# Attention and a gated MLP on one core: plain fp32 scores for the first three pairs, decode steps on GpSimd, and another written order

## The chip, the cores and the metric

The kernel runs on one core of a Trainium2 chip. The metric is the device time in microseconds of one execution; a profiled execution also gives its span, which begins and ends a little inside that time. On a core, TensorE (PE in the profile, PEld for its weight loads), VectorE (DVE), ScalarE (ACT) and GpSimd (POOL) each work through their own list of instructions in order and wait for one another by semaphores; SyncE (SP) issues nearly all transfers.

## The reference

For 8 batches and 8 heads, q, k and v have 576 positions of 64 numbers. q and k are rotated by position, scores are softmaxed, and the values are weighted; the heads of a batch then form the rows of a gated MLP with a product over positions.

```python
q_rot, k_rot = rotate(q), rotate(k)          # x1*cos - x2*sin, x1*sin + x2*cos
scores = q_rot @ k_rot.T / sqrt(64)
attn = exp(scores - max) / (sum + 1e-9)
x = (attn @ v)  -> [batch, 576, 512]
h = relu(x @ w_in); u, v = halves of h
v_n = (v - mean) / sqrt(var + 1e-6)
gated = u * (w_spatial @ v_n + b_spatial)
out = gated @ w_out
```

The arrays w_in and w_out arrive as 64-bit floats, read as two 32-bit words.

## The kernel before

Work goes by pairs of heads, 32 in all, four to a batch. Every product that needs full precision is made of fp32r products (one instruction each) of a high part, a rounded copy, and a low part, the rest. The only plain fp32 products are those of the values.

A pair is prepared (`prepare`, lines 442 to 531): q and k (two tiles `st`) and v (`vr`) are loaded; q and k are multiplied by a rotation table (`rope`, L487; q and k have tables of their own, `tabs`, in different row orders) and summed (`rope_sum`, L491); ScalarE makes high parts (L370, `hq`; L503), VectorE or GpSimd low parts (L373, `lq`; L471, `lk`). Then transfers from SBUF to SBUF build stacks (`ks`, `qs`, `qz`) in which the high and the low part stand in the two halves of the rows, so that one product takes both. Twelve such transfers, 1.56 MB, belong to a pair.

`attention` (L535) makes nine score tiles of 128 rows (`scores`, tile number 8 holds the rest of both heads): four products a tile (six for tile 8), the row maximum on VectorE (`nmx`, L583), the exponential on ScalarE (`e`, L584), a transpose in blocks on VectorE (`tu`, L594). When all nine are there, the values (`pv`, L553) follow in three chunks of 48 products; the three together are called a session here. `tu` has one buffer, so the next pair's transposes wait for the end of a session. `normalise` brings the sums across by a small transfer (`rt`, `rb`) and writes the MLP's input `x`.

`mlp` makes four groups of products per batch, named `pa`, `pb`, `pc` and `pd`, which run between the scores and values of the next batch's pairs. `decode` (L378) turns a 512 KB block of 64-bit weights into a high and a low part, with six steps on VectorE and two on ScalarE; twelve blocks are decoded, early in the program.

The order on each engine isn't the order of the code. `Program.run` (L140) plays all operations through a list of costs, keys and buffer counts when the program is written, and writes each engine's instructions in the order in which that play starts them. Keys (`PREP`, `STAGE`, `DEC_V` and the like) and buffer counts (`SLOTS`) are the numbers that set it. Where TensorE has nothing in that play, up to a set time, `warm` (L803) writes an idle product of zeros.

## Time and profile before

| | us |
|---|---|
| runs, lowest, median, highest | 935.18, 938.51, 942.9 |
| profiled execution | 940.61 |
| its span | 938.8 |
| TensorE busy | 864.5 |
| VectorE busy | 599.9 |
| ScalarE busy | 484.7 |
| GpSimd busy | 483.1 |

A busy TensorE is not TensorE at its peak: matmuls overlap, warm products count, and part of the time the granted clock is lower. Shares over the whole span hide that the program has stages; the rows below are by stage. Pairs and tiles are counted from 0. "Scores of pair 6" start at 194.72 us: they are the first split products after 194.32 in the timeline, and the place of each pair was read by laying the written order of TensorE beside the timeline.

### The profile page before, as it was taken

What the parts mean: (1) busy time and instruction counts of PE and PEld (TensorE: products, weight loads), DVE (VectorE), ACT (ScalarE), POOL (GpSimd) and SP (SyncE); (2) the same over time, 40 slices, a digit from 0 to 9 for tenths busy, and PEclk for the clock granted to TensorE, in tenths of its full rate; (3) what the DMA queues carried; (4) which work ended last, traced back from release to release, by engine and by line L of the source; (5) the groups of instructions that cost most, each with busy time, mean ns of one, the idle gap of its engine ahead of it and who ended that gap; (6) DMA issues with size and microseconds to landing.
All of it is one profiled execution on the core that took longest, in us unless ns stands there. A gap on an engine that the chain in (4) does not pass through costs nothing.

```text
span 938.8 us, 32216 instructions
## 1 busy us (share of the span) xinstructions
PE 864.5 (92%) x13594; PEld 762.6 (81%) x13594; DVE 599.9 (64%) x1203; ACT 484.7 (52%) x1207; POOL 483.1 (51%) x467
## 2 busy tenths in 40 slices
PE   7879867789889999999999999999999899999998
PEld 4656546689788988889988998799888899898998
DVE  3868778767658775675758665777557565965121
ACT  1434436554446644575457555674457445753352
POOL 1744235865545664675645574467466464423131
PEclk9879859999999999999999999999999999999999
DMA  9977978677888777877887789777877769663101
GB/s 228 246 170 197 212 180 201 149 176 173 187 210 208 165 171 200 194 175 164 189 213 178 176 189 233 157 182 177 205 184 168 164 151 238 139 139 72 52 1 51
DMA packets 101682, 161.13 MB, mean 172 GB/s; under 512 B 29153, under 2 KB 47969, under 8 KB 101538
## 3 DMA queue, kind: packets, MB, share of 16 engines
q1 hardware_dynamic: 100882, 157.82, 70.7%
q8 instruction: 107, 1.75, 0.8%
q10 hardware_dynamic: 656, 1.25, 0.5%
q14 instruction: 37, 0.30, 0.1%
HBM read 98.08 MB, written 9.96 MB: 115 GB/s over the span
## 4 chain that ended last, share of the span: by engine, by line
PE 68%; DMA 18%; DVE 5%; issue 4%; SPq 3%; ACT 1%; ACTq 0%; DVEq 0%
PE sc L579 15%; PE pv L553 14%; PE pc L712 10%; PE pb L694 9%; PE pd L732 9%; PE pa L671 8%; PE warm L806 3%; DMA qz<-hq 3%; DMA qs<-hq 3%; SPq L367 3%; DMA vr<-in_v_dram 1%; DVE tu L594 1%; DVE nmx L583 1%; DMA ks<-st 1%; DMA wi10raw<-in_w_in_dram 1%
## 5 line engine op out<-in xcount | busy, mean ns | idle before, releaser
L583 DVE TENSOR_REDUCE nmx<-sc 128x1 f32<-128x576 f32 x288 | 212.8, 744 | 153.6 <-PE sc L579 146.4
L584 ACT ACTIVATE e<-sc,nmx 128x576 f32<-128x576 f32 x288 | 212.7, 739 | 186.3 <-DVE nmx L583 149.9
L594 DVE STREAM_TRANSPOSE tu<-e 128x576 f32<-128x576 f32 x288 | 213.8, 759 | 35.0 <-PE pv L553 28.9
L487 POOL TENSOR_TENSOR st<-st,tabs 128x576 f32<-128x576 f32 x123 | 172.2, 1422 | 73.8 <-DMA st<-in_qk_dram 41.7
L553 PE MATMUL pv<-tu,vr 32*64 32x144 f32 x9216 | 182.9, 291 | 25.9 <-issue 25.0
L553 PEld LDWEIGHTS pv<-tu,vr 32*64 32x64 f32 x9216 | 150.5, 132 | 50.8 <-issue 46.1
L579 PE MATMUL sc<-ks,qs 128*128 128x288 f32 x640 | 145.1, 317 | 40.9 <-DVE x L630 15.8
L579 PEld LDWEIGHTS sc<-ks,qs 128*128 128x128 f32 x640 | 107.8, 197 | 63.2 <-issue 33.9
L579 PE MATMUL sc<-lk,qz 128*128 128x288 f32 x576 | 129.2, 307 | 1.5 <-DMA qz<-hq 1.3
L712 PE MATMUL pc<-wsp,vn 128*128 128x288 f32 x768 | 125.2, 298 | 0.2 <-ACT u L697 0.2
L671 PE MATMUL pa<-wi,x 128*128 128x512 f32 x448 | 121.2, 401 | 0.0
L694 PE MATMUL pb<-x,wi 128*128 128x288 f32 x768 | 119.8, 300 | 0.1
L373 POOL TENSOR_TENSOR lq<-st,hq 128x512 fp32r<-128x512 f32 (+1 forms) x62 | 51.0, 846 | 130.9 <-ACT hq L370 130.8
L373 POOL TENSOR_TENSOR x<-x,x 128x64 fp32r<-128x64 f32 (+1 forms) x96 | 59.4, 649 | 109.3 <-ACT x L370 109.3
L694 PEld LDWEIGHTS pb<-x,wi 128*128 128x128 f32 x768 | 108.5, 190 | 4.9 <-issue 3.4
L712 PEld LDWEIGHTS pc<-wsp,vn 128*128 128x128 f32 x768 | 109.8, 189 | 3.0 <-issue 2.6
L732 PE MATMUL pd<-g,wo 128*128 128x288 f32 x744 | 110.7, 298 | 0.0
L732 PEld LDWEIGHTS pd<-g,wo 128*128 128x128 f32 x744 | 103.0, 190 | 1.7 <-issue 1.6
L579 PEld LDWEIGHTS sc<-lk,qz 128*128 128x128 f32 x576 | 96.4, 197 | 3.5 <-DMA qz<-hq 3.3
L671 PEld LDWEIGHTS pa<-wi,x 128*128 128x128 f32 x448 | 79.5, 189 | 16.3 <-issue 4.0
L373 POOL TENSOR_TENSOR g<-u,g 128x288 fp32r<-128x288 f32 x64 | 52.7, 824 | 75.2 <-ACT g L370 75.1
L491 POOL TENSOR_TENSOR st<-st 128x576 f32<-128x576 f32 x62 | 87.9, 1420 | 4.0 <-DVE st L487 1.6
(104 smaller groups left out, 777.0 us busy)
## 6 DMA issues: line engine op xcount, KB each, us to landing
vr<-in_v_dram SPq DMA_DIRECT2D x128, 320.0 KB, 6.3
st<-in_qk_dram SPq DMA_DIRECT2D x32, 576.0 KB, 4.5
ks<-st SPq DMA_DIRECT2D x128, 144.0 KB, 5.6
qs<-hq SPq DMA_DIRECT2D x64, 164.0 KB, 5.1
qs<-lq SPq DMA_DIRECT2D x64, 164.0 KB, 6.2
st<-in_qk_dram SPq DMA_DIRECT2D x32, 288.0 KB, 4.0
out_dram<-ob SPq DMA_DIRECT2D x31, 288.0 KB, 3.7
st<-in_qk_dram SPq DMA_DIRECT2D x32, 256.0 KB, 4.4
```

The lines of the kernel that those rows point to most:

```text
L373: eng.tensor_tensor(out=lo, in0=src, in1=hi.bitcast(F32), op=ALU.subtract)
L487: f = lambda e: e.tensor_tensor(out=st[j][:, cols], in0=st[j][:, cols], in1=tabs[j][:, cols], op=ALU.mult)
L491: f = lambda e: e.tensor_tensor(out=st[j][:, :S], in0=st[j][:, :S], in1=st[j][:, S:2 * S], op=ALU.add)
L553: nc.tensor.matmul(outs[g][64 * a:64 * a + 64], lhsT=vr[rows, NQ * (kb % 4) + kb // 4, a, :], rhs=tu[rows, kb, Q4 * a:Q4 * a + Q4], start= ...
L579: nc.tensor.matmul(pt[:, n_c * 512:n_c * 512 + HALF], lhsT=lhsT, rhs=rhs[:, n_c * HALF:n_c * HALF + HALF], start=(n == 0), stop=(n == len( ...
L583: op(DVE, 749, key + k_max, lambda: nc.vector.tensor_reduce(out=nmx.tile, in_=tops(pt), op=ALU.max, axis=AX.XY, negate=True), r=[pt], w=[n ...
L584: op(ACT, 920, key + k_exp, lambda: nc.scalar.activation(e.tile.rearrange("p (c n) -> p c n", c=2), tops(pt), AF.Exp, bias=nmx.tile, scale ...
L594: nc.vector.transpose(out=dst, in_=src)
L671: nc.tensor.matmul(pm[:, :HF], lhsT=lhsT, rhs=win[1, d][:, j, :], start=(d == 0 and n == 0), stop=(d == 3 and n == len(todo) - 1))
L694: nc.tensor.matmul(pm[:, :HALF], lhsT=win[0, d][:, i, f * P:(f + 1) * P], rhs=x[d][:, at:at + HALF], start=(d == 0 and n == 0), stop=(d == ...
L712: nc.tensor.matmul(pm[:, :HALF], lhsT=lhsT, rhs=rhs, start=(t == 0 and n == 0), stop=(t == 4 and n == 1))
L732: nc.tensor.matmul(pm[:, :HALF], lhsT=wout[d,][:, i, m * P:(m + 1) * P], rhs=gs[d][:, at:at + HALF], start=(d == 0 and n == 0), stop=(d == ...
```

## The change

The first three pairs make no high and low parts and no stacks: the sum of the rotation writes q in fp32 straight into `hq` or `lq` in turn (and the columns of tile 8 into a new tile `jq`), ScalarE scales k in place, and a score tile is two plain fp32 products. `decode` has four steps on VectorE, three on ScalarE and two that GpSimd takes. q and k use one table. Between the chunks of a session of the first six pairs stand ten products of zeros. The planner knows sizes of transfers, `stage` and `e` have four buffers, `x32` goes into `rb`, and nearly all keys have other values.

```diff
-    "stage": 3, "lk": 2, "vraw": 1, "e": 3, "tu": 1, "rb": 1, "x32": 1, "xg": 7, "m": 4,
+    "stage": 4, "lk": 2, "vraw": 1, "e": 4, "tu": 1, "rb": 1, "xg": 7, "m": 4,
-DEC_V = [-26.92, 52.32, 24.86, 22.99]
+DEC_V = [650.29, 522.41, -36.97, 219.03]
+DEC_DVE = [0.0, 0.0]
+PLAIN = 3
+FILL_PAIRS, FILL = 6, 10
-WARM_FROM, WARM_FULL, WARM_TO, WARM_NS, WARM_AFTER, WARM_COLS = 2500, 44958.22, 100000, 170, -0.15, 384
+WARM_FROM, WARM_FULL, WARM_TO, WARM_NS, WARM_AFTER, WARM_COLS = 2500, 44958.22, 200000, 170, -0.15, 384
...
+                    if e == DMA and item[2].kb in (512, 576) and moved > now + FULL:
+                        passed.append(item)
+                        heapq.heappush(events, (moved - FULL, n, "wake", None))
...
-    tabs = [T([P, 2 * S], F32, f"tabs{j}") for j in range(2)]
+    tab2 = T([P, 2 * S], F32, "tab2")
+    jq = T([P, 2, P], F32, "jq")
...
-        op(DVE, 640, key - DEC_ON, bits(0xFFFFF, 0x100000, ALU.bitwise_and, ALU.bitwise_or), r=[t1], w=[pt])
-        op(DVE, 640, key - DEC_ON, lambda: stt(out=pt.tile, in0=word(0, U32), scalar=2.0**-32, in1=ints(), op0=ALU.mult, op1=ALU.add), r=[t0], w=[pt])
-        op(DVE, 640, key - DEC_ON, lambda: stt(out=pt.tile, in0=pt.tile, scalar=2.0**-20, in1=sg.tile.bitcast(F32), op0=ALU.mult, op1=ALU.mult), r=[sg], w=[pt])
-        op(ACT, 480, key - DEC_ON, high, r=[pt], w=[t0, t1, (n, "hi")])
-        op(DVE, 640, key - DEC_ON, lambda: rest_lo(nc.vector, where[at][:, 1, :], pt.tile, where[at][:, 0, :]), r=[pt, (n, "hi")], w=[n])
+        op(DVE, 640, key - DEC_ON, lambda: ts(out=ints(), in0=word(1), scalar1=0xFFFFF, scalar2=None, op0=ALU.bitwise_and), r=[t1], w=[pt])
+        op(ACT, 500, key - DEC_ON, lambda: nc.scalar.activation(pt.tile, ints(), AF.Copy, bias=1.0, scale=2.0**-20), w=[pt])
+        op(DVE, 640, key - DEC_ON, lambda: stt(out=val.tile, in0=word(0, U32), scalar=2.0**-52, in1=pt.tile, op0=ALU.mult, op1=ALU.add), r=[t0, pt], w=[val], new=[val])
+
+        def product(e):
+            e.tensor_tensor(out=val.tile, in0=val.tile, in1=sg.tile.bitcast(F32), op=ALU.mult)
+
+        prog.either({POOL: pool_ns(HF), **({DVE: 640} if DEC_DVE[0] > key else {})}, key - DEC_ON, lambda e: product(vec[e]), r=[sg], w=[val])
+        op(ACT, 480, key - DEC_ON, high, r=[val], w=[t0, t1, (n, "hi")])
+        prog.either({POOL: pool_ns(HF), **({DVE: 640} if DEC_DVE[1] > key else {})}, key - DEC_ON, lambda e: rest_lo(vec[e], where[at][:, 1, :], val.tile, where[at][:, 0, :]), r=[val, (n, "hi")], w=[n])
...
+        def plain_sum(e):
+            add = lambda **kw: e.tensor_tensor(op=ALU.add, **kw)
+            (dst, _), (x0, y0), (x1, y1) = spread((hq, lq)[i % 2].bitcast(F32)), turned(), turned(S)
+            add(out=dst, in0=x0, in1=x1)
+            for a in range(2):
+                rows = slice(64 * a, 64 * a + 64)
+                add(out=jq[rows, i % 2].rearrange("p (g n) -> p g n", n=32)[:, :, 16 * a:16 * a + 16], in0=y0[rows], in1=y1[rows])
...
+        if i < PLAIN:
+            scaled = lambda: nc.scalar.activation(st[1][:, :S], st[1][:, :S], AF.Copy, scale=0.125)
+            op(ACT, 573, key - K_HIQ, scaled, w=[(st[1], 0)])
+            prepped[i] = (lk, vr, st[1], i % 2)
+            return
...
+            if i < FILL_PAIRS and n < CHUNKS - 1:
+                for _ in range(FILL):
+                    nc.tensor.matmul(pv[1][:, Q4:Q4 + WARM_COLS - 16], lhsT=zero[:, :P], rhs=zero[:, 16:], start=False, stop=False)
...
+            if kt:
+                pq = (hq, lq)[n_q].bitcast(F32)
+                rows = slice(0, P) if c == 8 else slice(64 * heads[0], 64 * heads[0] + 64)
+                parts = [(jq[:, n_q] if c == 8 else pq[rows, P * (c % 4):P * (c % 4) + P], kt[rows, :S])]
```

Because the order is planned, the change moves instructions everywhere. Three places follow. In the names the number behind a letter group is the pair, the batch or the weight block (`st1_0` is q of pair 1, `wi02` block 2 of the first half of w_in); the last number counts buffers.

SyncE's queue at the start of the program, before, behind the load of pair 0's q:

```order
L367 DMA st0_1_98<-in_qk_dram 128x1152
L367 DMA vr0_120<-in_v_dram 32x4x640 x4
L367 DMA wi10raw_182<-in_w_in_dram 128x1024
L352 DMA st1_0_220<-in_qk_dram 64x1152
L353 DMA st1_0_220<-in_qk_dram 64x2x512
L354 DMA st1_0_220<-in_qk_dram 64x2x64
L367 DMA ks_76<-st0_1_98 64x576 x2
L367 DMA qs_75<-hq_78 64x656
L367 DMA qz_77<-hq_78 64x656
L367 DMA qs_75<-lq_79 64x656 x2
```

After, in the same place:

```order
L371 DMA st0_1_102<-in_qk_dram 64x1152
L372 DMA st0_1_102<-in_qk_dram 64x2x512
L373 DMA st0_1_102<-in_qk_dram 64x2x64
L386 DMA vr0_124<-in_v_dram 32x4x640 x4
L371 DMA st1_0_157<-in_qk_dram 64x1152
L372 DMA st1_0_157<-in_qk_dram 64x2x512
L373 DMA st1_0_157<-in_qk_dram 64x2x64
L371 DMA st1_1_183<-in_qk_dram 64x1152
L372 DMA st1_1_183<-in_qk_dram 64x2x512
L373 DMA st1_1_183<-in_qk_dram 64x2x64
```

The stacks of pair 0 and the first weight have gone from here, and the q and k of pair 1 and the q of pair 2 (the next rows) are loaded ahead of any weight.

VectorE while the first pair ends, before, with steps of the decode of `wi00` and `wi13`:

```order
L405 TENSOR_SCALAR dcwi13_599<-wi13raw_524 128x512
L413 SCALAR_TENSOR_TENSOR dcwi00_489<-wi00raw_427,dcwi00_489 128x512
L594 STREAM_TRANSPOSE tu0_376<-e0_7_601 128x18x32
L633 RECIPROCAL sums0_67<-sums0_67 128x9
L414 SCALAR_TENSOR_TENSOR dcwi00_489<-dcwi00_489,sgwi00_544 128x512
L634 STREAM_TRANSPOSE rt0_689<-sums0_67 128x32
L411 SCALAR_TENSOR_TENSOR sgwi13_693<-wi13raw_524,dcwi13_599 128x512
L373 TENSOR_TENSOR wi00_691<-dcwi00_489,wi00_691 128x512
```

After, GpSimd during the session of pair 0, with the last steps of the decode of `wi02`, `wi12` and `wi03`:

```order
L509 TENSOR_TENSOR st2_1_366<-st2_1_366,tab2_63 128x576 x2
L524 TENSOR_TENSOR st2_1_366<-st2_1_366 128x576
L437 TENSOR_TENSOR vlwi02_557<-vlwi02_557,sgwi02_477 128x512
L437 TENSOR_TENSOR vlwi12_566<-vlwi12_566,sgwi12_552 128x512
L392 TENSOR_TENSOR wi02_644<-vlwi02_557,wi02_644 128x512
L392 TENSOR_TENSOR wi12_647<-vlwi12_566,wi12_647 128x512
L509 TENSOR_TENSOR st3_0_432<-st3_0_432,tab2_63 128x576
L437 TENSOR_TENSOR vlwi03_713<-vlwi03_713,sgwi03_642 128x512
L524 TENSOR_TENSOR st3_0_432<-st3_0_432 128x576
L392 TENSOR_TENSOR x0_746<-rb0_635,x0_746 128x512
```

The product with the sign and power (L414 before, L437 after) and the low part (L373 before, L392 after) have moved from VectorE to GpSimd, where they stand between the rotations and sums (L509, L524) of pairs 2 and 3.

TensorE between the first and the second chunk of the session of pair 13, before, from the last products of one chunk to the first of the next:

```order
L553 MATMUL pv13_1_6016<-tu13_5844,vr13_5829 64x144
L553 MATMUL pv13_2_6017<-tu13_5844,vr13_5829 64x144 x2
L694 MATMUL pb2_00_6008<-x9_4562,wi01_2141 128x288 x3
L579 MATMUL sc14_2_6085<-ks_76,qs_75 128x288 x2
L579 MATMUL sc14_2_6085<-lk14_5543,qz_77 128x288 x2
L694 MATMUL pb2_00_6008<-x10_5003,wi02_2295 128x288 x3
L553 MATMUL pv13_0_6015<-tu13_5844,vr13_5829 64x144
```

After, between the second and the third chunk of the same session:

```order
L593 MATMUL pv13_1_5972<-tu13_5813,vr13_5795 64x144
L593 MATMUL pv13_2_5973<-tu13_5813,vr13_5795 64x144 x2
L747 MATMUL pb2_01_6070<-x9_4544,wi01_1369 128x288 x3
L628 MATMUL sc14_1_6143<-ks_75,qs_74 128x288 x2
L628 MATMUL sc14_1_6143<-lk14_5528,qz_76 128x288 x2
L747 MATMUL pb2_01_6070<-x10_4967,wi02_644 128x288 x3
L747 MATMUL pb2_10_6157<-x8_4098,wi00_1062 128x288 x3
L747 MATMUL pb2_01_6070<-x11_5554,wi03_754 128x288 x3
L747 MATMUL pb2_10_6157<-x9_4544,wi01_1369 128x288 x3
L593 MATMUL pv13_0_5971<-tu13_5813,vr13_5795 64x144
```

The first chunk's scores are now those of tile 0 of the next pair (tile 2 before), tile 1 stands in the second space, and more of the MLP's products stand between two chunks: 13 in the first space and 19 in this one, 10 in each before.

## Rows read from the trace of the kernel before

**Rows 1.** Stages: us; busy PE, PEld, DVE, ACT, POOL; clock; DMA share; GB/s.
```profile
0.00:26.39 26.39, 17.01 (x91) 9.56 (x92) 9.84 (x16) 3.89 (x6) 5.48 (x16) 0.92 0.96 227
26.39:194.72 168.33, 136.19 (x1963) 101.59 (x1964) 130.72 (x236) 82.02 (x192) 87.96 (x77) 0.85 0.80 193
194.72:275.00 80.28, 70.68 (x1234) 64.91 (x1233) 50.95 (x93) 38.88 (x101) 41.10 (x39) 0.98 0.79 187
275.00:870.00 595.00, 575.23 (x9862) 524.00 (x9861) 395.94 (x815) 334.55 (x848) 333.85 (x320) 0.99 0.75 177
```

**Rows 2.** TensorE's timeline: start, us, line, operation, tiles, count, idle before.
```profile
26.39 0.82 PE L579 MATMUL sc<-ks,qs 128*128 128x288 f32 x2 [8.25 <-DMA qs<-lq]
...
194.72 0.46 PE L579 MATMUL sc<-ks,qs 128*128 128x288 f32 x2
195.02 0.48 PE L579 MATMUL sc<-lk,qz 128*128 128x288 f32 x2
195.34 2.56 PE L694 MATMUL pb<-x,wi 128*128 128x288 f32 x18
```

**Rows 3.** Chain of work that ended last, before the first scores.
```profile
9.62 10.74 DMA wi10raw<-in_w_in_dram
...
22.57 3.69 DMA qs<-lq
```

**Rows 4.** VectorE's timeline, the first rotations.
```profile
9.70 1.43 DVE L487 TENSOR_TENSOR st<-st,tabs 128x576 f32<-128x576 f32 x2 [8.62 <-DMA tabs<-in_tab_dram]
12.99 1.43 DVE L487 TENSOR_TENSOR st<-st,tabs 128x576 f32<-128x576 f32 x2 [1.87 <-DMA tabs<-in_tab_dram]
```

**Rows 5.** Groups of instructions over the span, shapes kept apart.
```profile
L594 DVE STREAM_TRANSPOSE tu<-e 128x576 f32<-128x576 f32 x288 | 213.8, 759 | 35.0 <-PE pv L553 28.9 <-ACT e L584 5.8
...
L583 DVE TENSOR_REDUCE nmx<-sc 128x1 f32<-128x576 f32 x288 | 212.8, 744 | 153.6 <-PE sc L579 146.4 <-ACT g L370 5.9
...
L373 POOL TENSOR_TENSOR vn<-vv,vn 128x512 fp32r<-128x512 f32 x32 | 41.4, 1306 | 38.1 <-ACT vn L370 38.1
...
L373 DVE TENSOR_TENSOR wi<-dcwi,wi 128x512 fp32r<-128x512 f32 x8 | 5.4, 677 | 0.0
...
L410 ACT ACTIVATE dcwi<-dcwi,bias 128x512 int32<-128x512 int32 x8 | 5.3, 661 | 9.0 <-DVE dcwi L405 8.9
```

**Rows 6.** The table by stretch, four stretches of the second stage.
```profile
26.39:51.93 25.54, 23.65 (x310) 17.06 (x311) 22.26 (x35) 12.58 (x29) 15.70 (x13) 0.94 0.88 230
51.93:77.78 25.85, 22.61 (x188) 14.67 (x186) 17.78 (x29) 9.65 (x22) 11.13 (x11) 0.74 0.75 191
106.08:135.36 29.28, 18.05 (x341) 13.33 (x340) 22.37 (x38) 11.88 (x29) 9.76 (x10) 0.76 0.86 203
162.91:194.72 31.81, 27.02 (x406) 23.50 (x407) 22.71 (x58) 18.06 (x46) 25.47 (x21) 0.95 0.70 162
```

**Rows 7.** TensorE's timeline, session of values of pair 0.
```profile
50.80 1.20 PE L553 MATMUL pv<-tu,vr 32*64 32x144 f32 x53 [1.89 <-issue]
...
56.55 1.25 PE L553 MATMUL pv<-tu,vr 32*64 32x144 f32 x26 [2.44 <-issue]
```

**Rows 8.** TensorE's timeline, session of values of pair 13.
```profile
403.44 1.78 PE L553 MATMUL pv<-tu,vr 32*64 32x144 f32 x96
405.15 0.66 PE L694 MATMUL pb<-x,wi 128*128 128x288 f32 x3
...
409.00 0.46 PE L553 MATMUL pv<-tu,vr 32*64 32x144 f32 x2 [0.57 <-issue]
```

**Rows 9.** Waits at the values from 220 us on: total us, times, longest.
```profile
PE pv L553 <- issue: 10.9, 14, 2.0
...
PEld pv L553 <- issue: 28.8, 84, 2.3
```

**Rows 10.** The table by stretch: the session of pair 13 and the gap behind it.
```profile
403.44:412.68 9.24, 8.67 (x310) 7.48 (x309) 6.59 (x22) 8.06 (x21) 7.17 (x6) 1.00 0.63 162
412.68:429.50 16.82, 16.17 (x118) 15.58 (x117) 13.05 (x26) 11.70 (x29) 10.16 (x10) 1.00 0.88 184
```

More of the change, by code (lines that the diff above doesn't have):

```diff
@@ L116, in op, with move @@
         return self.either({eng: ns}, key, lambda e: f(), r, w, new, port, late)
+    def move(self, n, kb, key, f, **kw):
+        o = self.op(DMA, n * ISSUE, key, f, **kw)
+        o.kb = kb
+        return o
     def either(self, costs, key, f, r=(), w=(), new=(), port=True, late=0):
@@ L201, in run @@
                         if not a.waits:
-                            late = TO_PE if PE in a.costs and o.eng != PE else 0
+                            late = TO_PE if PE in a.costs and o.eng != PE else TO_DMA if DMA in a.costs and o.eng == PE else 0
                             heapq.heappush(events, (now + late, n, "ready", a))
@@ L233, in run @@
                     heapq.heappush(ready[e], item)
-                if e == PE and not chosen and max(WARM_FROM, idle + (WARM_AFTER if now > WARM_FULL else 0)) <= now < WARM_TO and free["pm"] and not kept:
+                if e == PE and not chosen and max(WARM_FROM, idle + (WARM_AFTER if now > WARM_FULL else 0)) <= now < WARM_TO and len(free["pm"]) > 2 * kept:
                     chosen = warm()
@@ L254, in run @@
                         chosen.costs[PE] = int(t - now)
+                    if e == DMA and chosen.kb:
+                        moved = max(moved, now + ISSUE) + int(chosen.kb * PER_KB)
+                        chosen.late += max(0, moved - now - chosen.costs[e])
                     for b in chosen.new:
@@ L401, in high @@
             where[at] = sb.tile([P, 2, HF], F32R, tag=n, name=n, bufs=1)
-            round_hi(where[at][:, 0, :], pt.tile)
+            round_hi(where[at][:, 0, :], val.tile)
         def bits(s1, s2, op0, op1):
@@ L407, in decode @@
         t0, t1 = (tok, 0), (tok, 1)
-        op(DMA, 2200, key - 8, fetch, w=[t0, t1])
+        prog.move(1, 512, key - 8, fetch, w=[t0, t1])
         op(DVE, 640, key, bits(20, 0x7FF, ALU.logical_shift_right, ALU.bitwise_and), r=[t1], w=[pt], new=[pt])
@@ L432, in fetch @@
             load(st[64:65, 1, :], b_sp)
-        op(DMA, 2000, key - 8, fetch, w=[st], new=[st])
+        prog.move(3, 290, key - 8, fetch, w=[st], new=[st])
         op(POOL, 2500, key, setup_moe, w=["ones", ("wt2", 0)], port=True)
@@ L473, in get @@
         def get(j):
-            if j:
-                load(st[j].tile, qk[b, hp, j].rearrange("p c n -> p (c n)"))
-            else:
-                unroll(st[j].tile, qk[b, hp, j], nc.sync)
+            unroll(st[j].tile, qk[b, hp, j], nc.sync)
         def get_v():
@@ L494, in prepare @@
         for j in range(2):
-            op(DMA, 2030, key - K_LOAD, lambda j=j: get(j), w=[(st[j], 0), (st[j], 1)], new=[st[j]], late=LATE_LOAD)
-        op(DMA, 4500, key - K_LOAD + 1, get_v, w=[vr], new=[vr])
+            prog.move(3, 511, key - K_LOAD, lambda j=j: get(j), w=[(st[j], 0), (st[j], 1)], new=[st[j]], late=LATE_LOAD)
+        prog.move(4, 1280, key - K_LOAD + 1, get_v, w=[vr], new=[vr])
         for j in range(2):
@@ L561, in tops, with scores @@
         return pt.tile.rearrange("p (c n) -> p c n", c=2)[:, :, :HALF]
-    def scores(i, c, lk, sm, key, k_max, k_exp, k_turn, tu, first):
+    def scores(i, c, lk, kt, n_q, sm, key, k_max, k_exp, k_turn, tu, first):
         pt = Buf("sc", None, None, f"sc{i}_{c}")
@@ L634, in normalise @@
         op(DVE, 125, key + K_INV, lambda: nc.vector.transpose(out=rt.tile, in_=sm), r=need, w=[rt], new=[rt])
[L635 to L637 removed]
+        prog.move(1, 16, key + K_INV, put, r=[rt], w=[(rt, 1)], late=300)
+        prog.move(3, 320, key + K_GET, get, r=[(rt, 1)], w=[rb], new=[rb], late=300)
+        op(DVE, dve_ns(S) + 220, key + K_X, scale, r=pv, w=[rb])
         op(ACT, 660, key + K_XHI, high, r=[x32, *([("gated", i // NP - 1)] if i >= NP and i % NP == NP - 1 else [])], w=[(x, 0)], new=[x])
@@ L735, in mlp @@
                 op(ACT, act_ns(HALF), key + K_OB, lambda ob=ob, pm=pm, c0=c0: nc.scalar.activation(ob[:, c0:c0 + HALF], pm[:, :HALF], AF.Copy), r=[pm, *[(ob, 0)][:c]], w=[(ob, c)], new=[ob] if c == 0 else [])
-            op(DMA, 800, key + K_OUT, lambda m=m, ob=ob: load(out[b, m * P:(m + 1) * P, :], ob.tile), r=[(ob, 0), (ob, 1)])
+            prog.move(1, 288, key + K_OUT, lambda m=m, ob=ob: load(out[b, m * P:(m + 1) * P, :], ob.tile), r=[(ob, 0), (ob, 1)])
     def last(gs, m, ob):
@@ L817, in tables @@
     def tables():
-        unroll(tabs[0], tab, nc.scalar)
-        nc.scalar.dma_start(out=tabs[1], in_=tab.rearrange("p c n -> p (c n)"))
+        unroll(tab2, tab, nc.scalar)
         nc.scalar.preload_act_table_set("natural_log_exp_and_others")
-    op(DMA, 100, -130, tables, w=[("tabs", 0), ("tabs", 1)])
+    prog.move(1, 576, -130, tables, w=["tab2"])
     prepare(0)
```

103 lines of the change are left out of this document (58 added, 45 removed).

## The prediction

> **What bounds the kernel now.** I read the stage table first, then the start and the end of the stage that looked wasteful, then the prices of single instructions, then the sessions of values. The program has three stages. Before the first scores TensorE only turns over idle products: 26.4 us [rows 1, 2]. From the first scores of pair 0 to the first scores of pair 6, at 194.72 us, the stage table shows TensorE busy for 136 of 168 us, but much of that is warm products, and the granted clock is 0.85, so part of the stage runs at 1.2 instead of 2.4 GHz [rows 1]. From there to the end, 744.1 us (938.8 - 194.72), TensorE is full: 575 of 595 us in the longest stretch at clock 0.99 [rows 1]. So the last stage is bound by TensorE's own work, and only its stalls can be had; what can really be won lies in the first 195 us.
>
> In the second stage no single engine is full. VectorE is busy 130.72 of 168.33 us (0.78), GpSimd 87.96 (0.52), and the DMA engines 0.80 of the time at 193 GB/s [rows 1]. VectorE is the one nearest to its limit: each of 54 score tiles costs it a maximum of 0.744 us and a transpose of 0.759 us, and 67 decode steps of about 0.68 us lie between them [rows 5]. Where its share drops, to 0.69 and 0.76, the granted clock is 0.74 and 0.76 as well; where the clock is 0.94 its share is 0.87 [rows 6]. I therefore take VectorE as the limit there, with the slow clock and late stacks as what keeps it waiting.
>
> **Part 1: the start, plain scores.** Today's first scores end a long row of steps. VectorE stands in order behind the load of the first weight, which took 10.74 us, so that the low part of q comes after it; the stack copy of that low part then takes 3.69 us more, and TensorE has waited 8.25 us for it [rows 2, 3]. With plain fp32 scores none of this is left: no split of q or k, no stacks, and in the order shown above no weight is ahead on VectorE. The new chain: the q product starts at 9.70 as now (it waits for table and q, which stay first in their queues) and two take 1.43; the sum in three pieces about 1.2 (one of 512 columns at 0.68, two small ones as an estimate); the k products 1.43, its sum 0.75; the scaling on ScalarE 0.68, close to the 0.66 of a 512-column step; 0.3 for hand-overs: 9.70 + 1.43 + 1.2 + 1.43 + 0.75 + 0.68 + 0.3 = 15.5 us [rows 4, 5]. The second table (576 KB) is not loaded any more. If k lands no earlier than now (12.99) it is 16.2; if everything lands 2.5 us sooner for the missing bytes, 13. I take 15.5, a gain of 10.9.
>
> The price of a plain product is not in this trace at this shape. A split product costs 2.56 us / 18 = 0.14 us [rows 2], the lower bound. The nearest row is the values, which are plain fp32: 48 products of 144 columns, each on an eighth of the array, in 1.71 us (403.44 to 405.15) [rows 8]; eight eighths and twice the columns make 0.57 us, the upper bound. A tile has two: 0.3 to 1.14 us. I take 1.0, near the row of the same type, against 0.57 for four split products (0.85 for the tile with six). That is 27 x 1.0 - 24 x 0.57 - 3 x 0.85 = +11 us for TensorE. They are hidden: VectorE needs 0.744 + 0.759 = 1.5 us for the same tile. At half clock a tile is 2.0 us, the cover is gone, and 27 tiles cost 13 us more; this stands in the upper end of the range.
>
> **Part 2: the second stage.** On VectorE the decode of a weight falls from six steps to four (the bit step, sign, mantissa and sum stay; the product and the low part go to GpSimd). Counted between the first scores of pair 0 and of pair 6 in the two orders, decode steps fall from 67 to 48; two k low parts fewer and two rotations more cancel. 19 x 0.68 = 13 us less: 117.7 us of VectorE work. At the present share of 0.78 this takes 151 us, at the best share above, 0.87, 135 us. I take 0.80, since ten idle products twice in each of the first six sessions, and warm products for longer, work against the dips of the clock: 147 us, and the first scores of pair 6 at 15.5 + 147 = 162.5 instead of 194.7. Bounds 150 and 167.
>
> TensorE's own load does not forbid it: in the written order 27 us of plain scores, 16 of split scores for three pairs, 26 of values (15 chunks of 48), 14 of the gated MLP, 177 warm and 100 idle products at 0.18 or less (50) make at most 133 of those 147 us.
>
> Transfers: by the first scores of pair 6 the queue moves 38.9 MB now and 34.0 MB after (three stacks of 1.56 MB and a table gone, a little more fetched ahead). At the present pace, 38.9 MB in 197 us, that is 172 us; at the 227 GB/s of the first stage, where the engines were 0.96 busy [rows 1], 150. The value 162.5 lies between the two, and needs 209 GB/s. The Trainium skill speaks against such a limit: its page "DMA: Bandwidth & Descriptors", section "Measured", gives 341 GB/s for a transfer of 1 MB, by which 34.0 MB would take an estimated 100 us and transfers would bound nothing. The trace does not agree: the engines were already 0.96 busy at 227.
>
> GpSimd gets what VectorE loses: 24 steps of 512 columns at 1.306 us, 31 us [rows 5]. Its work between the first rotation of pair 1 (about 13 us) and the low part of q of pair 6 adds up to some 114 us by the durations of rows of these shapes (1.42 us at 576 columns, 1.31 at 512). Its best share in a stretch now is 25.47 / 31.81 = 0.80 [rows 6]; at that it is done at 13 + 142 = 155, and with a stack copy of 3.7 us pair 6 can start at 159. So it fits, but with nothing to spare. ScalarE's third decode step, 12 x 0.66 = 8 us, lies in an engine that is busy 82 of 168 us [rows 1, 5], and costs nothing.
>
> **Part 3: the rest.** After that point the same work remains, with these differences. 48 products of the first gated MLP stand ahead of pair 6 now and 9 after: 39 x 0.14 = +5.5 us. The session of pair 5 holds 20 idle products of 368 columns, 0.18 us each by the split product's row scaled with the columns: +3.6. They fill the time in which a close session stands still: pair 0 lost 1.89 + 2.44 us at "issue", with nothing to wait for in the profile [rows 7]. I count both as cancelled, give or take 4. In the later pairs the chunks move apart: between two chunks there are 7 to 10 other products now, and mostly 13 to 24 after. In the session of pair 13 the second chunk lost 0.57 us at "issue" (409.00) [rows 8]. From 220 us on TensorE lost 10.9 us and its weight loads 28.8 us in this way at the values [rows 9]; these are the bounds of what stands still, 0 is the lower bound of what comes back, and I take 9. The last stage: 744.1 + 5.5 - 9 = 740.6.
>
> **Sum.** 162.5 + 740.6 = 903.1 us of span. The profiled execution took 940.61 with a span of 938.8, so 1.8 more, and lies 2.1 above the median of the runs, 938.51: 903.1 + 1.8 - 2.1 = 903 us.
>
> **Rivals.** (a) GpSimd takes VectorE's place in the second stage. Its queue runs in order, and a decode product that waits for VectorE holds back the rotations of later pairs, which hold back scores. For: over the stage its share is only 0.52 [rows 1], and it waits often for roundings. Against: it was short of work. At a share of 0.70 the low part of pair 6 is done at 13 + 163 = 176 and its scores start at 180: 903 + 17 = 920 us. (b) The same, worse, is the case that ends slower: at 0.60 it is 13 + 190 + 4 = 207, which is 903 + 44 = 947 us. It decides from about 0.64: then pair 6 starts at 195, as now. (c) The steady stage gives nothing back. A session becomes longer by its own spacing; VectorE can write the next transposes only when the values have been read, and in the gap after the session of pair 13 it is busy 13.05 of 16.82 us [rows 10]. For: the score maxima of the next tiles now stand right behind the session instead of before its first chunk. If the stalls stay (+9) and 25 pairs grow by 0.5 us (+12), the time is 924. (d) The second stage runs better than I say: VectorE at 0.87, transfers at 227 GB/s, pair 6 at 150, and all 20 us of stalls gone: 903 - 12 - 11 = 880. By the page's rate for transfers this case would come easier; the engines' 0.96 above holds it back. (e) The idle products don't keep the clock up, and plain scores run partly at half clock: up to +13, 916; this lies within the forecast's own range, 890 to 917.
>
> **Chances.** Forecast 0.60 (with e), a 0.15, b 0.05, c 0.08, d 0.12. The range reaches to a, c and d and leaves b out: 879 to 929. What a measurement of this kernel can tell from no change is about 1%, 929 to 948 here. Faster by more than 1%: the forecast, d, and nearly all of a and c: 0.87. Within 1%: 0.08, the late end of a and c and half of b. Slower: 0.05.
>
> **What would show it.** First scores at 15 to 16 us, with no weight ahead on VectorE. Plain score products with about 1 us a tile. First scores of pair 6 at 150 to 167, VectorE's share in that stage near 0.80, a granted clock above 0.85, and GpSimd's share near 0.75. Waits for "issue" at the values after 220 us below 20 us in the weight loads, and the time from pair 6 on at 735 to 750 us. The forecast is wrong if GpSimd is late (VectorE's and TensorE's waits then name its tiles or the stacks of q's low part), if the transposes at the end of a pair wait for VectorE so that values start late, or if the plain scores take TensorE longer than VectorE needs for a tile.

## The result and the profile after

| | before | after |
|---|---|---|
| median of 4 runs (lowest to highest), us | 936.85 (934.67 to 942.9) | 894.75 (890.15 to 902.29) |
| profiled execution, its span, us | 940.61, 938.8 | 894.36, 892.6 |
| first scores of pair 0 | 26.39 | 15.94 |
| from there to the first scores of pair 6 | 168.3 (to 194.72) | 155.3 (to 171.21) |
| from there to the end | 744.1 | 721.4 |

The ratio is 0.9549 with an interval of 0.9468 to 0.963, so the change makes the kernel 4.5% faster. I had said 903 us in 879 to 929. The 46.2 us of span come from all three stages: 10.4 us before the first scores, 13.1 in the second stage and 22.7 in the last. I had 10.9, 21.3 and 3.5. The sum was nearly right because two of its terms were wrong in opposite directions, and the experiments are about these two.

First the stage table of after, cut at its own marks. The columns are us of the window; busy us and count of PE, PEld, DVE, ACT, POOL; granted clock; DMA share; GB/s. It answers to [rows 1].

```profile
0.00:15.94 15.94, 12.39 (x59) 6.55 (x60) 4.87 (x9) 1.97 (x2) 4.07 (x15) 1.00 0.93 188
15.94:171.21 155.27, 144.44 (x2005) 97.27 (x2006) 117.30 (x198) 83.78 (x192) 116.64 (x101) 0.95 0.86 200
275.00:824.00 549.00, 541.42 (x9425) 498.35 (x9413) 373.05 (x777) 325.12 (x813) 310.48 (x299) 1.00 0.80 182
```

In the second stage VectorE's work is 117.30 us, which I had counted as 117.7. Its share is 0.755 and not 0.80. GpSimd's is 116.64 / 155.27 = 0.75. The six stretches of that stage answer to [rows 6]:

```profile
15.94:39.49 23.55, 23.55 (x78) 12.90 (x78) 13.51 (x19) 9.69 (x21) 11.90 (x11) 0.71 0.82 206
39.49:64.96 25.47, 24.78 (x375) 15.07 (x374) 22.64 (x39) 15.12 (x33) 23.89 (x22) 1.00 0.88 237
64.96:101.02 36.06, 33.93 (x600) 20.80 (x599) 32.13 (x55) 22.52 (x50) 31.31 (x26) 1.00 0.88 204
101.02:120.76 19.74, 15.51 (x174) 11.33 (x174) 14.92 (x24) 9.62 (x22) 18.34 (x17) 0.91 0.84 180
120.76:146.27 25.51, 23.78 (x398) 18.38 (x396) 18.91 (x35) 13.80 (x33) 18.23 (x16) 1.00 0.89 192
146.27:171.21 24.94, 22.88 (x388) 18.79 (x389) 15.20 (x30) 13.02 (x34) 12.99 (x12) 1.00 0.80 174
```

Three things stand out. Pair 0 runs at a mean clock of 0.71, and VectorE is busy only 0.57 of its stretch. Then GpSimd is nearly full: 0.94, 0.87 and 0.93 from 39.49 to 120.76 us; but VectorE is at 0.89 in the first two of these stretches, above the best share of before. From 120.76 us on both fall, VectorE to 0.68 and GpSimd to 0.62, at full clock. The timeline of TensorE shows what went before the slow clock, and the price of a plain tile (it answers to [rows 2]):

```profile
11.73 1.79 PE L859 MATMUL warm<-zero 128*128 128x384 bf16 x10
15.94 3.45 PE L628 MATMUL sc<-st,hq 64*128 64x288 f32 x8 [2.42 <-ACT st L535]
...
21.99 4.20 PE L628 MATMUL sc<-st,hq 64*128 64x288 f32 x8
...
33.65 2.20 PE L628 MATMUL sc<-st,hq 64*128 64x288 f32 x8
```

TensorE stood idle for 2.42 us ahead of the first scores. The granted clock then fell to its half level, 1.2 GHz: it is 0.50 from 18 to 30 us. Two plain tiles (eight instructions) take 2.20 us at full clock, 1.1 each; they took 3.45 right after the wait and 4.20 at half clock. Pair 3, the first with stacks, starts only at 101.02. The chain of waits ahead of it begins with the load of its q and k (columns: start, us, what):

```profile
77.23 9.32 DMA st<-in_qk_dram
...
86.71 2.79 POOL st L509 x2
...
89.57 1.41 POOL st L524
90.98 1.52 POOL lq L392 x2
92.50 2.47 POOL vlwi L437 x2
94.97 3.01 POOL wi L392 x2
```

Rotations, sum, low part and four decode steps stand in one row on GpSimd behind that load. The low part is ready at 92.50, but its copies stand behind other transfers in SyncE's row and are issued from 97.66 on, so the decode steps behind it do not explain their delay. In the written order pair 3's scores also stand behind two chunks of pair 2's values with their idle products, which end at 100.1, so in the end TensorE waited 0.85 us. In the last stage the waits from 220 us on answer to [rows 9] (total us, times, longest):

```profile
PE pv L593 <- issue: 4.6, 5, 1.7
PEld pv L593 <- issue: 19.9, 68, 2.0
```

Before these were 10.9 and 28.8. The whole last stage, first before, then after, shows how long TensorE was not busy:

```profile
194.72:938.80 744.08, 711.31 (x11542) 651.42 (x11540) 459.32 (x953) 398.74 (x1009) 389.67 (x375) 0.99 0.70 165
```

```profile
171.21:892.60 721.39, 708.09 (x11601) 652.84 (x11599) 456.80 (x977) 408.93 (x1020) 383.24 (x369) 1.00 0.74 169
```

That is 32.8 us before and 13.3 after. In before, TensorE's largest waits in this stage were these, of which only the first is at the values:

```profile
PE pv L553 <- issue: 13.4, 16, 2.0
PE sc L579 <- DVE x L630: 7.7, 7, 2.7
PE sc L579 <- DMA qs<-hq: 4.5, 2, 2.3
PE sc L579 <- DMA qz<-hq: 1.3, 2, 1.1
```

The second line is scores that wait for VectorE's scaling of the values, the last two are scores that wait for stack copies. After, the values wait 4.6 us, and no wait for the scaling is left. The session of pair 13 answers to [rows 8, 10]. Its chunks begin 3.6 and 4.4 us apart, and the first two take 1.71 us each:

```profile
374.70 1.78 PE L593 MATMUL pv<-tu,vr 32*64 32x144 f32 x96
376.41 0.66 PE L747 MATMUL pb<-x,wi 128*128 128x288 f32 x3
...
378.32 1.78 PE L593 MATMUL pv<-tu,vr 32*64 32x144 f32 x96
380.03 0.66 PE L747 MATMUL pb<-x,wi 128*128 128x288 f32 x3
...
382.74 1.78 PE L593 MATMUL pv<-tu,vr 32*64 32x144 f32 x96
```

### The profile page after: what moved, and what is told of

It is laid out like the page before. It is cut to its first block, busy times and chain, and to the rows that moved or that the text cites. A ratio compares the mean times of both kernels' runs of the same rounds, so it can differ in the third digit from the quotient of the medians.

```text
span 892.6 us, 32569 instructions
## 1 busy us (share of the span) xinstructions
PE 864.9 (97%) x13662; PEld 756.7 (85%) x13662; DVE 579.0 (65%) x1183; ACT 494.7 (55%) x1213; POOL 504.0 (56%) x485
## 4 chain that ended last, share of the span: by engine, by line
PE 77%; DMA 9%; POOL 5%; SPq 3%; issue 3%; ACT 2%; DVE 1%; ACTq 0%; POOLq 0%; DVEq 0%
PE sc L628 18%; PE pv L593 14%; PE pc L765 12%; PE pb L747 10%; PE pa L724 10%; PE pd L785 9%; DMA st<-in_qk_dram 4%; PE warm L859 3%; SPq L386 2%; DMA ks<-st 2%; POOL st L509 2%; DMA qs<-hq 1%; POOL st L524 1%; PE pv L597 1%; DMA qs<-lq 1%
## 5 line engine op out<-in xcount | busy, mean ns | idle before, releaser
L509 POOL TENSOR_TENSOR st<-st,tab 128x576 f32<-128x576 f32 x122 | 171.8, 1427 | 102.7 <-DMA st<-in_qk_dram 81.5
L647 DVE STREAM_TRANSPOSE tu<-e 128x576 f32<-128x576 f32 x288 | 216.7, 761 | 4.4 <-ACT e L637 4.4
L593 PE MATMUL pv<-tu,vr 32*64 32x144 f32 x9216 | 173.6, 287 | 5.2 <-issue 5.2
L593 PEld LDWEIGHTS pv<-tu,vr 32*64 32x64 f32 x9216 | 146.0, 130 | 28.0 <-issue 25.1
L628 PE MATMUL sc<-ks,qs 128*128 128x288 f32 x580 | 127.3, 309 | 12.6 <-ACT e L637 5.2
L628 PEld LDWEIGHTS sc<-ks,qs 128*128 128x128 f32 x580 | 93.6, 189 | 30.6 <-issue 9.4
L628 PE MATMUL sc<-lk,qz 128*128 128x288 f32 x522 | 112.2, 296 | 0.0
L524 POOL TENSOR_TENSOR st<-st 128x576 f32<-128x576 f32 x60 | 85.6, 1428 | 7.9 <-DMA st<-in_qk_dram 5.3
L392 POOL TENSOR_TENSOR lq<-st,hq 128x512 fp32r<-128x512 f32 (+1 forms) x58 | 45.6, 808 | 73.5 <-ACT hq L389 51.4
L392 POOL TENSOR_TENSOR g<-u,g 128x288 fp32r<-128x288 f32 x64 | 51.2, 807 | 63.2 <-ACT g L389 61.7
L628 PEld LDWEIGHTS sc<-lk,qz 128*128 128x128 f32 x522 | 84.1, 189 | 0.2 <-DMA qz<-hq 0.2
L392 POOL TENSOR_TENSOR x<-rb,x 128x64 fp32r<-128x64 f32 (+1 forms) x90 | 55.6, 648 | 46.5 <-ACT x L389 32.9
```

What stands on the lines that cost most here:

```text
L392: eng.tensor_tensor(out=lo, in0=src, in1=hi.bitcast(F32), op=ALU.subtract)
L509: f = lambda e: e.tensor_tensor(out=st[j][:, cols], in0=st[j][:, cols], in1=tab2[:, cols], op=ALU.mult)
L524: f = lambda e: e.tensor_tensor(out=st[j][:, :S], in0=st[j][:, :S], in1=st[j][:, S:2 * S], op=ALU.add)
L593: nc.tensor.matmul(outs[g][64 * a:64 * a + 64], lhsT=vr[rows, NQ * (at % 4) + at // 4, a, :], rhs=tu[rows, kb, Q4 * a:Q4 * a + Q4], start= ...
L628: nc.tensor.matmul(pt[:, n_c * 512:n_c * 512 + HALF], lhsT=lhsT, rhs=rhs[:, n_c * HALF:n_c * HALF + HALF], start=(n == 0), stop=(n == len( ...
L647: nc.vector.transpose(out=dst, in_=src)
```

## The experiments

Each kernel is the one after with the edit shown. "Pair 6" is the start of its first scores in the profiled execution, "rest" the time from there to the end of the span. Where an edit changes a key, a cost or a buffer, the program plans the whole order anew; where it only emits more or fewer instructions, the order of all others stays.

| run | median us | ratio to before (interval) | pair 6 | rest |
|---|---|---|---|---|
| after | 894.75 | 0.9549 (0.9468 to 0.963) | 171.2 | 721.4 |
| after_again | 893.27 | 0.9532 (0.9492 to 0.9571) | 167.7 | 723.0 |
| chunk_near | 934.49 | 0.9925 (0.989 to 0.9961) | 173.7 | 756.2 |
| close_mid | 930.74 | 0.9913 (0.9882 to 0.9944) | 171.6 | 757.8 |
| one_row_hold | 1014.29 | 1.0816 (1.0757 to 1.0876) | 165.5 | 842.5 |
| six_hold | 941.25 | 1.0028 (0.9992 to 1.0065) | 168.1 | 766.1 |
| e3 | 908.3 | 0.9639 (0.9609 to 0.967) | 179.3 | 728.3 |
| no_fill | 901.66 | 0.9574 (0.9539 to 0.9608) | 175.4 | 724.5 |
| hold | 891.32 | 0.9463 (0.943 to 0.9495) | 168.6 | 719.8 |
| hold_thin | 900.61 | 0.9621 (0.9577 to 0.9666) | 173.3 | 723.9 |
| plain0 | 915.8 | 0.9777 (0.9733 to 0.9822) | 185.9 | 728.4 |
| dec_prod | 914.87 | 0.9757 (0.9721 to 0.9794) | 181.6 | 731.5 |
| swap_hold | 901.4 | 0.9622 (0.9564 to 0.9681) | 176.1 | 723.4 |

**The last stage: chunks closer again (chunk_near).**

```diff
-STAGE = [-6.98, 1.13, 28.11, -195.61, 30.41, 4.09, 10.34]
+STAGE = [-6.98, 1.13, 28.11, -195.61, 30.41, 2.2, 10.34]
```

> The kernel after, with the key that spaces the chunks of the later pairs back to 2.2 from 4.09: between two chunks of a session of pair 6 and later stand 8 other products in the middle (16 after, 10 before). Up to the first scores of pair 6 the written order is the same. Theory 'spacing' (the last stage, which came out 23 us shorter than before, gained it mainly where the chunks of values moved apart and TensorE no longer stands still behind them): 895 + 10 to 15 = 905 to 910 us, and PE and PEld waits for 'issue' at the values after 200 us back near the 11 and 29 us of before. Theory 'buffers' (the gain came from the fourth buffer of exponentials, with which scores and values wait less for VectorE): within 3 us of 895.

The rest grew by 34.8 us, more than the change had won there. So the last stage of after needs the spacing, and for far more than the waits at "issue". It became even longer than before's (756.2 against 744.1), where 10 products stood between two chunks, so with close chunks other keys of after seem to cost time; what the spacing alone does in the kernel before was not tried. The waits from 220 us on:

```profile
PE sc L628 <- DVE rb L683: 17.2, 12, 3.1
PE pv L593 <- issue: 12.7, 18, 1.4
...
PEld pv L593 <- issue: 32.0, 90, 1.6
```

The larger part of these is scores that wait for VectorE's scaling of the values. The third accumulator of a session lies in one of the two PSUM buffers of the scores until then.

**Closer, with the middle of the session kept (close_mid).**

```diff
-STAGE = [-6.98, 1.13, 28.11, -195.61, 30.41, 4.09, 10.34]
+STAGE = [-6.98, 1.13, 28.11, -195.61, 30.41, 1.12, 13.3]
```

> The kernel after with the chunk key at 1.12 as before the change, and the session shifted so that its middle chunk keeps its place in the order (key of the values 13.3 instead of 10.34): 9 other products between two chunks in the middle (16 after, 8 in the run with key 2.2). That run lost 34.8 us in the last stage, 12 behind chunks at 'issue' and 21 by waits of scores, mostly for VectorE's scaling of the values (17.2 us), which holds one of the two PSUM buffers of the scores. Theory 'spacing' (close chunks leave too few scores between them, and the scaling comes when the next scores are due): last stage 745 to 760 us, waits of scores for the scaling over 8 us, time 920 to 935. Theory 'place' (the sessions ended too early against the next pair's scores, and with the middle kept the waits for the scaling go): last stage 725 to 735 us, time 900 to 910.

The time fits "spacing" (rest +36.4), its mechanism does not: the waits for the scaling are nearly gone, as "place" said, and a little under half of the loss now stands at the values. Of the other half 13 us are longer busy time of TensorE (721.3 against 708.1 from pair 6 on), which the trace does not explain.

```profile
PE pv L593 <- issue: 20.0, 15, 3.2
...
PE sc L628 <- DVE rb L683: 0.9, 1, 0.9
...
PEld pv L593 <- issue: 37.8, 85, 3.5
```

**One row of 144 products, all else in its place (one_row_hold).** With 15 idle products as in hold, below.

```diff
+        def row(n):
+            if i < FIRST:
+                values(n)
+            elif n == CHUNKS - 1:
+                for j in range(CHUNKS):
+                    values(j)
...
-lambda n=n: values(n)
+lambda n=n: row(n)
```

> The kernel with 15 idle products ahead of the first scores, in the same order, but from pair 6 on the three chunks of a pair's values stand in one row of 144 products at the place of the third chunk; everything else, scores and gated MLP, keeps its place. That takes away the spacing without moving the end of a session, which the runs with other keys did not separate (they lost 35 and 36 us in the last stage, one mostly with scores waiting for VectorE's scaling, the other with values at 'issue'). Theory 'row' (TensorE stands still at 'issue' when rows of values products follow closely, whatever stands around them): the last stage grows from 719.8 us by 25 to 70, the waits of PE and PEld for 'issue' at the values after 200 us go from 4.4 and 20 us to over 15 and 35. Theory 'order' (close chunks lost because the other work around them was moved): last stage within 8 us of 719.8, or up to 10 us shorter, since 52 changes between values and other products fall away. Up to pair 6 nothing differs, so its first scores at 166 to 171 us show once more what the clock does in pair 0.

The rest grew by 122.7 us, 4.7 per pair, beyond what "row" said. In the session of pair 13 (timeline of TensorE, then its waits from 220 to 870 us):

```profile
410.29 3.90 PE L593 MATMUL pv<-tu,vr 32*64 32x144 f32 x231
415.98 1.22 PE L593 MATMUL pv<-tu,vr 32*64 32x144 f32 x57 [1.80 <-issue]
417.14 0.54 PE L638 MATMUL sc<-ks,qs 128*128 128x288 f32 x2
```

```profile
PE pv L593 <- issue: 66.1, 24, 4.7
PE sc L638 <- ACT e L647: 18.3, 22, 1.8
```

The row takes 417.14 - 410.29 = 6.85 us where three single chunks take 5.13. It is one of the shorter ones: by the timeline the 26 rows take from 5.9 to 11.4 us and 226 us together, 92 more than 78 single chunks. Since no other instruction changed its place in the order, these stalls belong to the row itself. Scores lose too, waiting for exponentials, and the mean clock of 275 to 940 us falls to 0.95; what the clock has to do with the longer rows was not separated. "Order" falls.

**Six chunks of 24 (six_hold).** With the 15 idle products.

```diff
+        ch = CHUNKS if i < FIRST else 6
+        if i >= FIRST:
+            K_CHUNK = 1.64
...
-        for n in range(CHUNKS):
+        for n in range(ch):
```

> The kernel with 15 idle products ahead of the first scores, and from pair 6 on the values of a pair in six chunks of 24 products over the same stretch of the order instead of three of 48 (8 other products between two chunks in the middle instead of 16). Its last stage was 719.8 us with three chunks; TensorE's loss against the sum of its products' own times in it was 35 us, 10 of them behind chunks of values, and 70 to 72 in the two runs with close chunks. Theory 'density' (what stands still at 'issue' grows with the length of a row of values products without others between): last stage 705 to 717 us, waits of PEld for 'issue' at the values below 15 us. Theory 'distance' (what counts is the time between the end of one chunk and the start of the next, 2 to 4 us with three chunks, about half with six): last stage 725 to 750 us. Third: a change between values and other products costs 0.1 us each, 75 x 2 more of them: +8 to +15 us, without more waits at 'issue'.

All three theories missed the size: the rest is 46.3 us longer than in hold. A chunk of 24 products takes not half of 1.71 us but 0.97, and the waits at the values are many and short:

```profile
385.07 1.04 PE L597 MATMUL pv<-tu,vr 32*64 32x144 f32 x48
386.04 0.54 PE L635 MATMUL sc<-ks,qs 128*128 128x288 f32 x2
```

```profile
PE sc L635 <- ACT e L644: 7.7, 5, 3.6
...
PEld pv L597 <- issue: 28.8, 136, 1.2
```

"Density" falls. A chunk thus has a price of its own, 2 x 0.97 - 1.71 = 0.23 us, and three more of them in 26 pairs make 18 us; the rest of the 46 was not separated further.

**Three buffers of exponentials (e3).**

```diff
-    "stage": 4, "lk": 2, "vraw": 1, "e": 4, "tu": 1, "rb": 1, "xg": 7, "m": 4,
+    "stage": 4, "lk": 2, "vraw": 1, "e": 3, "tu": 1, "rb": 1, "xg": 7, "m": 4,
```

> The kernel after with three buffers of exponentials instead of four (the rule that ties the later tiles of a pair to the first values of the pair before moves with it); spacing of the chunks as after (15 other products in the middle). Theory 'spacing': within 4 us of 895. Theory 'buffers': 895 + 10 to 20 = 905 to 915 us, with waits of scores for VectorE or ScalarE back in the last stage, where after has a last stage of 721 us and before one of 744.

The time, 908.3 us, is the one that "buffers" gave, but more than half of the loss lies ahead of pair 6: the rest is 6.9 us longer and pair 6 8.1 us later. The waits of scores that "buffers" expected in the last stage hardly grew: for exponentials 4.3 us from 200 us on, against 2.6. The fourth buffer has a share, in both stages, but spacing without it keeps most of the last stage's gain.

**Idle products between chunks left out (no_fill).**

```diff
-                for _ in range(FILL):
+                for _ in range(0):
```

> The kernel after in the same order with the idle products between the chunks of the first six sessions left out (100 products before the first scores of pair 6, 20 in the session of pair 5); nothing of the result changes. Theory 'fill' (my prediction: they stand where TensorE would stand still at 'issue' anyway, so they cost about nothing, and they keep the clock up): 895 to 905 us, with 1.5 to 4 us of 'issue' in each of the first sessions instead of the idle products, or a lower granted clock behind a session. Rival 'cost' (TensorE is the bound of the first six sessions, and 120 products of 0.17 us are 20 us of its time): 877 to 888 us.

"Fill" holds by its time. Though 100 x 0.17 = 17 us of TensorE's work is gone ahead of pair 6, pair 6 comes 4.2 us later in this profile, and the stage runs at clock 0.87 (after 0.95):

```profile
15.80:175.40 159.60, 140.89 (x1904) 96.39 (x1905) 118.71 (x198) 84.16 (x192) 116.11 (x101) 0.87 0.84 195
```

From 40 us on the clock is 0.90, against 0.99 in after and 0.96 in after_again. The 4.2 us at pair 6 are little more than the 3.5 us between two executions of after. By the ratios, whose intervals overlap, it is the same or slightly slower.

**Idle products into the wait ahead of pair 0 (hold), half of the later warm products left out (hold_thin), after once more (after_again).**

```diff
+            if i == 0 and first:
+                for _ in range(15):
+                    nc.tensor.matmul(pt[:, :WARM_COLS], lhsT=zero[:, :P], rhs=zero, start=True, stop=True)
```

In hold_thin, of the warm products after the 61st every second one is not emitted:

```diff
+        count.append(b)
+        keep = len(count) <= 61 or len(count) % 2
```

> The kernel after with 15 more idle products right ahead of the first scores, in the 2.4 us in which TensorE now waits for the scaled k of pair 0 (13.5 to 15.9 us); after that wait the granted clock falls to 0.5 until about 30 us, and pair 0's scores take 23.6 us. Theory 'clock' (that wait costs the clock, and the clock costs pair 0 its time): the clock stays 1.0 at 16 to 30 us, pair 1 starts its scores 5 to 8 us earlier than 39.5 us, and the whole takes 887 to 892 us. Rival 'supply' (pair 0's speed does not matter, since the loads of the next pairs and GpSimd's rotations set when pair 3 and pair 6 can start): the clock is held, the first scores of pair 6 stay within 1.5 us of 171.2, and the time within 2 us of 895. Third outcome: the clock falls nevertheless, and nothing changes.

> The kernel with 15 idle products ahead of the first scores, and of the 177 warm products that follow the first scores every second one left out (88 remain), in the same order otherwise; nothing of the result changes. With all of them and the clock held, pair 0 to 2 have 5 to 11 warm products between two tiles, and they stand in the chain of waits with 16.7% of 20 to 171 us. Theory 'cost' (they take TensorE's time where scores could already run): pair 3 2 to 5 us earlier than 98.2, pair 6 2 to 6 us earlier than 168.6, time 880 to 887 us by the clock of the runs of this kernel (ratio 0.935 to 0.943). Theory 'clock' (without them TensorE idles and the clock falls): mean granted clock of the stage below 0.93, pair 6 later than 170, ratio 0.95 to 0.96. Rival 'supply' (loads and GpSimd set the pace): within 2 us of the kernel with all of them.

> The kernel after once more, unchanged, on the chip of the two runs beside it, so that their times can be compared with it to less than one per cent: ratio to before 0.950 to 0.960, first scores of pair 1 near 39.5 us and of pair 6 near 171 us with the granted clock at 0.5 from 18 to 30 us.

One window of each, 16 to 40 us, first hold, then hold_thin, then after_again:

```profile
16.00:40.00 24.00, 24.00 (x198) 14.32 (x199) 20.13 (x31) 13.42 (x30) 18.85 (x17) 1.00 1.06 251
```

```profile
16.00:40.00 24.00, 23.80 (x58) 12.46 (x58) 13.38 (x19) 9.84 (x22) 11.68 (x11) 0.56 0.83 203
```

```profile
16.00:40.00 24.00, 23.98 (x189) 13.85 (x189) 18.66 (x28) 12.54 (x29) 17.08 (x16) 0.93 1.02 245
```

With the wait filled the clock held, and pair 1 started at 32.86 instead of 39.49 us, as "clock" said. The median, 891.32 us, lies in the range of "clock" too. But of these 6.6 us only 2.6 are left at pair 6, so most of them are taken up on the way, as "supply" had argued, though beyond its 1.5. After_again missed its expectation: the same program lost the clock for less long (0.93) and reached pair 6 at 167.7, although TensorE waited 3.81 us ahead of its first scores, longer than the 2.42 of after. In after, chunk_near and close_mid, which are the same up to there, the window shows 0.72; in six_hold and one_row_hold, with the idle products and a wait of about 1.2 us left, 0.93 and 0.93; in swap_hold, with no wait left, 1.00 as in hold. So the loss differs between executions and does not follow the length of the wait alone; where the wait was wholly filled, both executions kept the clock. Hold is the fastest version here, by 0.7 to 0.9% in the ratios and 0.2 to 0.4% in the medians; its interval overlaps with those of after and after_again, so the gain is not settled. In hold_thin the clock is lost again (0.83 from 16 to 168 us, 0.99 in hold), pair 6 is 4.7 us later, and "cost" falls: the warm products pay for their time.

**Stacks for all pairs (plain0).** `PLAIN = 3` becomes 0.

> The kernel after with the first three pairs' scores split and stacked again, as all others; one table, decode split, spacing and idle products as after. Theory 'start' (plain scores are worth the 11 us by which the first scores come earlier, and the stacks' transfers behind it): first scores at 22 to 27 us instead of 15.9, first scores of pair 6 5 to 12 us later than 171.2, last stage within 5 us of 721, time 901 to 909 us (ratio to before about 0.965). Rival 'handover' (the change from plain to split scores before pair 3, where after has no scores from 89.6 to 101.0 us, gives the 11 us back): pair 6 within 3 us of 171, time within 4 us of after.

"Handover" falls, and the price is twice what "start" gave: first scores at 32.09, pair 6 14.7 us later, the rest 7.0 longer. The chain ahead of the first scores:

```profile
10.01 7.70 DMA vr<-in_v_dram
...
17.73 6.50 DMA wst<-in_w_spT_dram
...
25.72 0.69 ACT st L542
...
27.79 4.29 DMA ks<-st
...
32.09 2.02 PE sc L628 x7
```

The new order put a weight ahead of k's split on ScalarE, as before had one ahead of q's on VectorE [rows 3]. So a part of the 16 us is that order's and not the stacks'; how much was not tried.

**One decode step back on VectorE (dec_prod).** The product's choice of engines becomes `{DVE: 640}`.

> The kernel after with one of the two decode steps, the product, back on VectorE for all 12 weights (12 x 0.68 us more there, 12 x 1.3 us less on GpSimd, which after keeps busy 0.87 to 0.94 of the time from 39 to 121 us, against VectorE's 0.75 to 0.89). Theory 'GpSimd bound' (rival a of my prediction holds in part): pair 3 starts earlier than 101 us, pair 6 2 to 6 us earlier than 171.2. Theory 'VectorE bound': pair 6 3 to 9 us later. 48 products more of one kind of the gated MLP (24 of them of its second part) can stand ahead of pair 6 in the new order, which is 3 us of TensorE's time that the last stage has less.

Pair 3 came 2.2 us earlier, but pair 6 10.4 later: "VectorE bound" fits in its sign and is passed in size, and "GpSimd bound" holds only up to pair 3. VectorE has 125.79 us to do up to 181.57 us against 117.30, but its share stays at 0.76, so the run does not show that VectorE is the limit. Fifteen more products of the gated MLP, not 48, stand ahead of pair 6.

```profile
15.60:181.57 165.97, 151.24 (x2009) 101.37 (x2010) 125.79 (x213) 85.38 (x193) 104.68 (x91) 0.92 0.78 185
```

**The tiles of plain q exchanged (swap_hold).** `(hq, lq)` becomes `(lq, hq)` for the plain pairs; 15 idle products as in hold.

> The kernel with 15 idle products ahead of the first scores (three us faster than after by the median) and the two tiles that hold the plain q exchanged: pair 2's plain q then lies in the tile of the low part, and the high part of pair 3's split q need not wait for pair 2's last plain scores. In after ScalarE waits with that split until 89.7 us, its four stack copies run from 91.6 to about 97.7, and pair 3's first scores stand at 101.0 us (98.2 with the idle products). Theory 'shared tile': pair 3's first scores at 92 to 96 us, pair 6's 2 to 5 us earlier than 168.6, time 884 to 889 us. Rival 'loads' (q and k of pair 3 land only at 86.5 us, and GpSimd has rotations, sums and decode steps to make after that): pair 3 within 1.5 us of 98, time as with the idle products alone.

Both missed: the copies of pair 3's low part were issued at 91.37 us instead of 94.86 in hold (97.66 in after), but its scores stand behind two chunks of pair 2 as in hold. These began 3.3 us later than there, since 79 to 93 us ran at clock 0.68 (1.00 in hold), and the second lost 2.17 us at "issue" (1.12): pair 3 at 102.6 instead of 98.2. I had not taken that place of the order into account. What the shared tile costs is not settled by this.

## Why the prediction was right in sum and wrong in two terms

- **Start.** Right: 15.94 against 15.5. The steps are those of the sum, on the same engines, with no weight ahead; the first began 0.7 us later than I had it (10.40, when the table had landed), and the steps behind it took 0.3 less.
- **Plain tile.** Right: 1.1 us at full clock against 1.0. The case that I had put into the range only, plain tiles at half clock (e), came for pair 0. I had read [rows 2] for its wait and its prices, but not asked what the new wait ahead of the first scores does to the clock.
- **Second stage, 147 us.** Mis-sized: 155.3 (151.7 in after_again, 167.72 - 16.02). The work on VectorE was right to 0.4 us, the share 0.80 was not reached. At 0.80 throughout, pair 0's stretch would have been 6.7 us shorter, the two to 101 us 7.0 longer, the next 1.1 shorter and the two from 120.76 us on 7.8 shorter. So the shortfall lies at both ends and not where GpSimd is nearly full. Pair 0's clock is worth 3 us or so of it at pair 6. In the last 50 us two stack copies of q stand in the chain of waits:

```profile
135.02 9.09 DMA qs<-lq
...
144.12 4.99 DMA qs<-hq
```

ScalarE wrote the next high part of q at 149.56, behind these copies, and GpSimd stood still for it for 9.0 us. That the copies set the pace there is argued from these rows and not shown by a run. Rival (a) had pair 6 at 180, the forecast at 162.5, and 171.2 and 167.7 lie between; but the rows do not show its mechanism, decode products on GpSimd that hold back the scores, as what cost this time. GpSimd's share came out at 0.75 as said. In dec_prod, giving a step back to VectorE was worse.
- **Transfers.** 34.0 MB by 162.5 us needed 209 GB/s; the stage ran at 200, with the DMA engines 0.86 busy.
- **Idle products.** Right: counted as cancelled, and no_fill is within a few us. The lower clock without them, 0.90 against 0.96 to 0.99 from 40 us on, fits the second reason that I gave.
- **Last stage, "I take 9".** This is the term that failed. The rest is 721.4 instead of 740.6. With 5.5 us more work than before in it, some 28 us came back. At the values themselves 8.8 us did (13.4 to 4.6), close to the 9. The other 19 I had put at nothing: the waits of scores for the scaling (7.7 us) and for stack copies (5.8) are gone, other waits of TensorE grew by some 3, and some 9 us lie in TensorE's busy time, which nothing here separates; the clock, 0.99 before and 1.00 after, could make up to an estimated 7 of them (1% of 711). My own [rows 1] had TensorE idle for 29.4 us from 194.72 to 870 us, and I asked only for the values' part. That the stage needs the chunks' spacing is shown: undoing it cost 34.8 and 36.4 us, one row 122.7. With close chunks the next scores can come due while the session's accumulator still holds a score buffer: 17.2 us in chunk_near, and the 7.7 us in before. That the spacing alone made the stage shorter is not shown, since other keys of the last stage, the fourth buffer of exponentials (6.9 us in e3) and the rest of the planned order changed with it. Rival (c), a stage that grows with its longer sessions, did not come: a session takes 10.5 us on the mean of the 26, against 9.0 before, but the gap behind it 14.2 against 16.5.

## What to carry to other kernels

When many small products of one kind stand in a row, look at what stands still behind the row and who holds a buffer meanwhile, and price both: the waits of TensorE at the row itself were a quarter to a half of the loss here. When you price what a stage can give back, start from all of its idle time and name every wait in it; here a third of the gain stood in the wait that was priced. Idle products paid for their time here because the engine would have waited there anyway; look for the wait just ahead of a stage too, not only for the mean clock. When a sum is right, check each of its terms: two of these were off by 8 and 19 us.
